# The experts' sums of the last chunk: from one VectorE instruction to ScalarE and GpSimd

## The chip, the cores and the metric

The kernel runs on one core of a Trainium2 chip. The metric is device time in microseconds (us) of one execution, smaller is better. Engines are named as the profile names them: PE (TensorE), DVE (VectorE), ACT (ScalarE), POOL (GpSimd), SP (SyncE, which here only issues DMAs). Each engine works through its own queue in order, and waits on semaphores for the others.

## The reference

Three stages. A top-32 attention (2 batches, 8 heads, 576 positions, head size 64) gives 1152 rows of 512. Then come four experts, all computed for every row and weighted by a normalised gate, and then a layer with three first matrices whose products are maximised:

```python
p = domain_probs / (domain_probs.sum(-1, keepdims=True) + 1e-09)
out = np.zeros((N, D))                      # N, D = 1152, 512; E = 4; F = 1024
for e in range(E):
    h = np.maximum(x @ w1[e], 0.0)
    out += p[:, e:e + 1] * (h @ w2[e])
...
h = np.maximum(np.maximum(x @ w1, x @ w2), x @ w3)     # d_ff = 768
return (h @ w_out).astype(np.float32)
```

The change is in the line `out += p * (h @ w2)`. The last stage's four matrices arrive as float64.

## The kernel before, in words

The 1152 rows are nine tiles of 128, in four chunks: `CHUNKS = [[0, 1], [2, 3], [4, 5], [6, 7, 8]]`. The work runs in eight phases, `PHASES`: the experts of chunks 0 to 3, then the last layer of chunks 0 to 3. The attention of later chunks goes on beside the first three expert phases. When the experts of chunk 3 (the last chunk, three tiles, N = 384 columns) run, it has ended.

**Experts.** An expert's 1024 hidden units are worked on in halves i = 0 to 7 (two halves to an expert). For each half PE makes two first products (`half1`, u = 0 and 1, 24 matmuls of 384 columns each into two PSUM banks); ACT takes them out with the ReLU into `hh`, DVE writes the remainder `hl` (L668, L670; every fourth goes over ACT and POOL, L661 to L663). Then `half2` multiplies with the second matrix: for each of the three tiles 12 matmuls of 512 columns into a PSUM tile `ps2` of the pool `po`, which has two buffers. So the third tile of a half (and the first tile of the next) can only begin when the buffer of two tiles earlier has been read out. The order on PE is first products of i+1, second products of i, and so on. Below, "step" is one such pair: 48 matmuls of 384 columns and 36 of 512.

What reads `ps2` out in the last chunk: for i = 0 ACT copies it with the gate's factor into `acc` (L692, three instructions). For i = 1 to 7 DVE does `acc = ps * gate + acc` in one instruction (L699), 3 x 7 = 21 of them. `ON_POOL_E = (0, 1)` keeps a third way (L693 to L696) switched off. In the chunks with two tiles both halves of an expert are added up in PSUM, and the same L699 runs once per expert and tile.

**Order of the instructions.** The read-outs are put on a list by `later()`; each later read-out first lets every waiting one issue its next stage (`tick`), so a read-out of two stages issues its second instruction when the next but one is put on the list. Nothing reorders afterwards: the order in which the program issues is the order on each engine.

**Weights.** Every 128x1024 block of weights is loaded by SP (L176), split by ACT into a high part `whi` (L225) and by POOL or DVE into the remainder `wlo` (L231). In the last chunk and the phases after it the blocks alternate: one on POOL (two instructions of 128x512), one on DVE (one of 128x1024). There are five buffers of each part; `weight()` splits up to four blocks ahead.

**Conversion.** Beside all this the four float64 matrices are turned into float32, in 48 pieces of 128x256 (`to_float32`). A piece takes two ACT instructions (L196, L197), three DVE instructions (L199, L202, L205), one POOL addition of int32 (L208), and an ACT-issued DMA that stores it (L213, `narrow`); five buffers circulate for the raw and five for the finished piece. The loads of the next phase's weights read what was stored.

**What sets how conversion and expert work interleave.** The program keeps two counters, `clock["dve"]` and `clock["pe"]`, of DVE and PE work issued so far. Per slot of the attention and conversion schedule, PE work is issued until it has caught up with the DVE work issued. Each L699 is counted there by `dve(DM)`, 0.07 + 512/960 = 0.60 us:

```python
                dve(DM)
                stages = [lambda: nc.vector.scalar_tensor_tensor(out=acc[ti], in0=ps, scalar=g, in1=acc[ti], op0=ALU.mult, op1=ALU.add)]
```

After the experts of chunk 3 comes the last layer of chunk 0 (phase 4), whose first products (216 matmuls of 256 columns) need the turned sums `x2h`, `x2l` of chunk 0 (L747 on PE, L752 on ACT, L753 on DVE) and the split weights.

Of the kernel before, what the change touches and what calls it, by code (L numbers as in the profile page):

```python
# [10 lines left out]
F32 = mybir.dt.float32  # L11
# [9 lines left out]
BEGIN, READY = 4, 4  # L21
SPLIT_K, SPLIT_Q = 8, 10
ON_POOL_H = 4
ON_POOL_E = (0, 1)
H_LAG, E_LAG = 0, 0
WAITING = 3
PAUSE = 0.8
# [23 lines left out]
def kernel(  # L51
# [15 lines left out]
    B, HP, D, _, S = k.shape  # L67
    NT, DM = out.shape
    E = gates.shape[2]
    P = 128  # L70
# [11 lines left out]
    MAXT = max(len(x) for x in CHUNKS)  # L82

    SLOTS = [[(t, b) for t in x for b in ((0, 1) if t == MIXED else (0 if t < MIXED else 1,))] for x in CHUNKS]
    MAXS = max(len(x) for x in SLOTS)
# [3 lines left out]
    kv = ctx.enter_context(tc.tile_pool(name="kv", bufs=2))  # L89
    qp = ctx.enter_context(tc.tile_pool(name="qp", bufs=2))  # L90
# [4 lines left out]
    ms = ctx.enter_context(tc.tile_pool(name="ms", bufs=2))  # L95
# [546 lines left out]
    def experts(n, c):  # L642
# [36 lines left out]
        def half2(i, ti, hs):  # L679
            begin, end = (not i % 2, i % 2 == 1) if whole else (True, True)  # L680
            if begin:
                outs[ti] = po.tile([P, DM], F32, tag="o", name="ps2")
            ps = outs[ti]
            assert {("h", n, i, 0), ("h", n, i, 1)} <= made
            yield from layer2(ps, [weight((c, "b", i, u), (c, "b", i, 0)) for u in range(2)], hs, N, ti, begin, end)
            if not end:
                return

            g = gate[:, tiles[ti], i // 2:i // 2 + 1]
            made_e[0] += 1  # L690
            if i < 1 + whole:
                stages = [lambda: nc.scalar.activation(out=acc[ti], in_=ps, func=AF.Copy, scale=g)]  # L692
            elif made_e[0] % ON_POOL_E[1] < ON_POOL_E[0]:  # L693
                tmp = ms.tile([P, 2 * MAXT * P], F32, tag="tm", bufs=2, name="tmp")[:, 0:DM]
                stages = [lambda: nc.scalar.activation(out=tmp, in_=ps, func=AF.Copy, scale=g),
                          lambda: nc.gpsimd.tensor_tensor(out=acc[ti], in0=acc[ti], in1=tmp, op=ALU.add)]  # L696
            else:
                dve(DM)
                stages = [lambda: nc.vector.scalar_tensor_tensor(out=acc[ti], in0=ps, scalar=g, in1=acc[ti], op0=ALU.mult, op1=ALU.add)]  # L699
            if i == 2 * E - 1:  # L700
                final = stages.pop()
                stages.append(lambda: [final(), made.add(("acc", c, ti))])
            later(*[lambda: None] * E_LAG, *stages)
# [213 lines left out]
```

## Time and profile before

| | us |
|---|---|
| median of the runs shown (3 runs, 794.56 to 802.54) | 795.2 |
| the profiled execution, own time | 795.39 |
| its span, first to last instruction | 793.6 |
| PE busy in the span | 737.1 (93%) |
| DVE busy | 666.1 (84%) |
| POOL busy | 557.5 (70%) |
| ACT busy | 492.8 (62%) |
| last chunk's experts, first to last matmul | 488.10 to 629.96 |

The own time is 1.8 us longer than the span. A PE that is busy need not be at its peak, since consecutive matmuls overlap in the records. The useful number is the distance between starts: about 0.17 us for 384 columns and 0.23 us for 512 in the last chunk.

### The profile page before, as it was taken

How to read it: one execution, taken by the hardware profiler on the slowest of the kernel's cores; microseconds unless marked ns; L12 is line 12 of the kernel's file. 1: busy time of each engine (PE TensorE's matmuls, PEld its weight loads, DVE VectorE, ACT ScalarE, POOL GpSimd, SP SyncE). 2: the span in 40 equal slices, each digit the busy share in tenths (PEclk: the TensorE clock that was granted, in tenths of full speed). 3: DMA queues.
4: the chain of work that ended last, by engine and by line, in shares of the span. 5: the costliest groups of instructions: out<-in, count | busy, mean ns of one | idle time of the engine just before them, and what ended most of it. 6: DMA issues, size and time to landing. Idle time of an engine off the chain costs nothing.

```text
span 793.6 us, 14150 instructions
## 1 busy us (share of the span) xinstructions
PE 737.1 (93%) x4942; PEld 656.4 (83%) x4942; DVE 666.1 (84%) x1242; ACT 492.8 (62%) x1027; POOL 557.5 (70%) x452
## 2 busy tenths in 40 slices
PE   3776799889999999999999999999999899999998
PEld 2554699788898988888888988889988797989996
DVE  6999999999999999999999996889999773434341
ACT  5666768577786776777777765755654444544541
POOL 2787988779888978778878785677465574655430
PEclk9976799999999999999999999999999999999999
DMA  3430155535555446354543465968877554656431
GB/s 99 119 108 4 52 166 153 173 112 165 161 178 154 141 146 176 99 162 132 158 133 130 136 196 169 282 220 269 248 248 243 167 171 174 213 186 208 166 104 41
DMA packets 50216, 126.26 MB, mean 159 GB/s; under 512 B 7904, under 2 KB 18144, under 8 KB 50144
## 3 DMA queue, kind: packets, MB, share of 16 engines
q1 hardware_dynamic: 41936, 116.69, 48.0%
q10 hardware_dynamic: 8208, 8.65, 3.1%
q8 instruction: 39, 0.64, 0.3%
q14 instruction: 33, 0.27, 0.1%
HBM read 116.67 MB, written 8.65 MB: 158 GB/s over the span
## 4 chain that ended last, share of the span: by engine, by line
DVE 44%; PE 33%; DMA 8%; issue 6%; POOL 4%; ACT 4%; SPq 1%; ACTq 0%; DVEq 0%; POOLq 0%
DVE m L372 16%; DVE work L374 14%; PE ps L590 8%; PE ps L592 8%; PE ps L591 8%; DVE p L392 6%; POOL wlo L231 3%; DMA raw<-in_w_dram 2%; ACT whi L225 2%; DMA raw<-narrow 2%; DVE h L670 2%; PE pso L592 1%; PE pso L590 1%; DMA raw<-in_m_dram 1%; PE pso L591 1%
## 5 line engine op out<-in xcount | busy, mean ns | idle before, releaser
L231 POOL TENSOR_TENSOR wlo<-raw,whi 128x512 fp32r<-128x512 f32 x272 | 374.9, 1406 | 140.2 <-ACT whi L225 129.0
L225 ACT ACTIVATE whi<-raw 128x1024 fp32r<-128x1024 f32 x176 | 182.8, 1057 | 76.2 <-PE ps L592 25.2
L590 PE MATMUL ps<-xl,whi 128*128 128x256 f32 (+1 forms) x512 | 154.2, 301 | 0.5 <-DVE h L670 0.5
L372 DVE MAX8 m<-work 128x8 f32<-128x576 f32 x216 | 154.4, 741 | 0.1
L592 PE MATMUL ps<-xh,wlo 128*128 128x256 f32 (+1 forms) x512 | 151.8, 296 | 0.0
L591 PE MATMUL ps<-xh,whi 128*128 128x256 f32 (+1 forms) x512 | 151.7, 296 | 0.0
L231 DVE TENSOR_TENSOR wlo<-raw,whi 128x1024 fp32r<-128x1024 f32 x40 | 57.4, 1435 | 76.5 <-ACT whi L225 71.9
L374 DVE MATCH_REPLACE8 work<-m,work 128x576 f32<-128x576 f32 x144 | 106.2, 738 | 0.0
L590 PEld LDWEIGHTS ps<-xl,whi 128*128 128x128 f32 x512 | 97.7, 191 | 1.6 <-DVE h L670 0.7
L591 PEld LDWEIGHTS ps<-xh,whi 128*128 128x128 f32 x512 | 97.8, 191 | 0.9
L592 PEld LDWEIGHTS ps<-xh,wlo 128*128 128x128 f32 x512 | 97.7, 191 | 0.0
L592 PE MATMUL ps<-x2h,wlo 128*128 128x256 f32 (+1 forms) x288 | 85.4, 297 | 0.8 <-DVE wlo L231 0.8
L590 PE MATMUL ps<-x2l,whi 128*128 128x256 f32 (+1 forms) x288 | 85.2, 296 | 0.0
L591 PE MATMUL ps<-x2h,whi 128*128 128x256 f32 (+1 forms) x288 | 85.2, 296 | 0.0
L590 PE MATMUL ps<-wlo,h 128*128 128x512 f32 x192 | 77.8, 405 | 0.0
L592 PE MATMUL ps<-whi,h 128*128 128x512 f32 x192 | 75.3, 392 | 0.0
L591 PE MATMUL ps<-whi,h 128*128 128x512 f32 x192 | 75.3, 392 | 0.0
L392 DVE SCALAR_TENSOR_TENSOR p<-s,m,p 128x576 f32<-128x576 f32 x57 | 73.4, 1288 | 0.0
L410 PE MATMUL psp<-ident,p 128*128 128x128 f32 x288 | 49.4, 299 | 24.1 <-POOL p L396 15.4
L351 PE MATMUL pss<-kT,ql 128*128 128x288 f32 x160 | 55.0, 358 | 13.5 <-DVE ql L295 7.5
L208 POOL TENSOR_TENSOR narrow<-narrow,raw 128x256 int32<-128x256 int32 x48 | 41.4, 863 | 33.7 <-DVE narrow L205 9.6
L410 PEld LDWEIGHTS psp<-ident,p 128*128 128x128 f32 x288 | 37.4, 153 | 30.3 <-POOL p L396 18.8
(104 smaller groups left out, 1682.1 us busy)
## 6 DMA issues: line engine op xcount, KB each, us to landing
raw<-in_w_dram SPq DMA_DIRECT2D x128, 512.0 KB, 3.8
raw<-narrow SPq DMA_DIRECT2D x48, 512.0 KB, 3.5
raw<-in_m_dram SPq DMA_DIRECT2D x36, 256.0 KB, 4.6
narrow<-narrow ACTq DMA_DIRECT2D x48, 128.0 KB, 3.9
kraw<-in_k_dram SPq DMA_DIRECT2D x14, 288.0 KB, 4.3
raw<-in_mo_dram SPq DMA_DIRECT2D x12, 256.0 KB, 4.0
vt<-in_v_dram SPq DMA_DIRECT2D x8, 288.0 KB, 4.3
out_dram<-ob ACTq DMA_DIRECT2D x9, 256.0 KB, 2.1
```

What stands on the lines that cost most here:

```text
L208: nc.gpsimd.tensor_tensor(out=out.bitcast(I32), in0=out.bitcast(I32), in1=last, op=ALU.add)
L225: nc.scalar.activation(out=hi, in_=raw, func=AF.Copy)
L231: on.tensor_tensor(out=lo[:, x], in0=raw[:, x], in1=hi[:, x].bitcast(F32), op=ALU.subtract)
L351: nc.tensor.matmul(ps[:, 0:SH], lhsT=l, rhs=r, start=i == 0, stop=i == len(mm) - 1)
L372: nc.vector.max(m[:, 8 * r:8 * r + 8], src)
L374: nc.vector.match_replace(out=self.w[j], in_to_replace=m[:, 8 * r:8 * r + 8], in_values=src, imm_value=NEG)
L392: nc.vector.scalar_tensor_tensor(out=p, in0=s, scalar=kth, in1=p, op0=ALU.is_ge, op1=ALU.mult, accum_out=total)
L410: nc.tensor.transpose(ps[:, r * P:(r + 1) * P], self.p[:, part, part * TAIL + r * P:part * TAIL + (r + 1) * P], ident)
L590: nc.tensor.matmul(ps, lhsT=lh, rhs=rl, start=first, stop=False)
L591: nc.tensor.matmul(ps, lhsT=lh, rhs=rh, start=False, stop=False)
L592: nc.tensor.matmul(ps, lhsT=ll, rhs=rh, start=False, stop=last)
L670: lambda: [nc.vector.scalar_tensor_tensor(out=hl[:, g], in0=ps, scalar=0.0, in1=hh[:, g].bitcast(F32), op0=ALU.max, op1=ALU.subtract) for ...
```

## The change

For the last chunk (`not whole`), i = 1 to 7, the one DVE instruction is replaced by two. ACT takes the product out of PSUM with the gate's factor into `tmp`, and POOL adds `tmp` to `acc`. `tmp` alternates between two tiles, those in which the attention loaded its raw q and raw k (one buffer each). `dve(DM)` is not called on this path.

```diff
@@ -21,7 +21,6 @@
 BEGIN, READY = 4, 4
 SPLIT_K, SPLIT_Q = 8, 10
 ON_POOL_H = 4
-ON_POOL_E = (0, 1)
 H_LAG, E_LAG = 0, 0
@@ -690,8 +689,10 @@
             made_e[0] += 1
             if i < 1 + whole:
                 stages = [lambda: nc.scalar.activation(out=acc[ti], in_=ps, func=AF.Copy, scale=g)]
-            elif made_e[0] % ON_POOL_E[1] < ON_POOL_E[0]:
-                tmp = ms.tile([P, 2 * MAXT * P], F32, tag="tm", bufs=2, name="tmp")[:, 0:DM]
+            elif not whole:
+
+                tmp = (qp.tile([P, 2, MAXS * P], F32, tag="qraw", bufs=1, name="tmp") if made_e[0] % 2 else
+                       kv.tile([P, 2, S], F32, tag="kraw", bufs=1, name="tmp")).rearrange("p a n -> p (a n)")[:, 0:DM]
                 stages = [lambda: nc.scalar.activation(out=tmp, in_=ps, func=AF.Copy, scale=g),
                           lambda: nc.gpsimd.tensor_tensor(out=acc[ti], in0=acc[ti], in1=tmp, op=ALU.add)]
             else:
```

PE's order stays as it was, row for row. On the others, two kinds of thing move: the read-out itself, and, because the counter of DVE work now grows more slowly, the conversion's pieces relative to the expert work. Line numbers of the changed kernel are one lower than before up to the change, and one higher behind it.

The queue of ACT at the read-outs of i = 1. `whi` is a weight's high part, `narrow` and `raw64` a piece of the conversion, `hh` a hidden block, `ps2` the product. Before:

```order
L668 ACTIVATE hh_6730<-ps1_6717 128x384
L213 DMA narrow3_101<-narrow_6664 128x256
L196 ACTIVATE narrow_6802<-raw64_6734 128x256
L197 ACTIVATE raw64_6734<-raw64_6734 128x256
L213 DMA narrow3_101<-narrow_6689 128x256
L225 ACTIVATE whi_6815<-raw_6697 128x1024
L225 ACTIVATE whi_6822<-raw_6746 128x1024
```

And now:

```order
L667 ACTIVATE hh_6730<-ps1_6717 128x384
L212 DMA narrow3_101<-narrow_6664 128x256
L195 ACTIVATE narrow_6793<-raw64_6734 128x256
L196 ACTIVATE raw64_6734<-raw64_6734 128x256
L696 ACTIVATE tmp_6770<-ps2_6741,gate_95 128x512
L212 DMA narrow3_101<-narrow_6689 128x256
L195 ACTIVATE narrow_6820<-raw64_6763 128x256
L196 ACTIVATE raw64_6763<-raw64_6763 128x256
L696 ACTIVATE tmp_6796<-ps2_6773,gate_95 128x512
L224 ACTIVATE whi_6826<-raw_6697 128x1024
L224 ACTIVATE whi_6833<-raw_6746 128x1024
L696 ACTIVATE tmp_6823<-ps2_6800,gate_95 128x512
```

The three read-outs now stand in ACT's queue, the first behind a store of the conversion and a piece's two instructions, and the two `whi` stand behind the second.

POOL's queue in the same step, from the remainder of the weight that is loaded as `raw_6697` on. Before:

```order
L231 TENSOR_TENSOR wlo_6816<-raw_6697,whi_6815 128x512 x2
L208 TENSOR_TENSOR narrow_6767<-narrow_6767,raw64_6685 128x256
L231 TENSOR_TENSOR wlo_6868<-raw_6820,whi_6867 128x512 x2
L208 TENSOR_TENSOR narrow_6802<-narrow_6802,raw64_6734 128x256
L208 TENSOR_TENSOR narrow_6846<-narrow_6846,raw64_6763 128x256
L208 TENSOR_TENSOR narrow_6893<-narrow_6893,raw64_6798 128x256
L208 TENSOR_TENSOR narrow_6921<-narrow_6921,raw64_6842 128x256
L663 TENSOR_TENSOR hl_6913<-raw_6914,hh_6912 128x768
```

And now:

```order
L697 TENSOR_TENSOR acc_6341<-acc_6341,tmp_6770 128x512
L230 TENSOR_TENSOR wlo_6827<-raw_6697,whi_6826 128x512 x2
L697 TENSOR_TENSOR acc_6342<-acc_6342,tmp_6796 128x512
L207 TENSOR_TENSOR narrow_6793<-narrow_6793,raw64_6734 128x256
L697 TENSOR_TENSOR acc_6343<-acc_6343,tmp_6823 128x512
L230 TENSOR_TENSOR wlo_6884<-raw_6831,whi_6883 128x512 x2
L207 TENSOR_TENSOR narrow_6820<-narrow_6820,raw64_6763 128x256
L207 TENSOR_TENSOR narrow_6861<-narrow_6861,raw64_6789 128x256
L207 TENSOR_TENSOR narrow_6909<-narrow_6909,raw64_6816 128x256
L207 TENSOR_TENSOR narrow_6950<-narrow_6950,raw64_6857 128x256
L662 TENSOR_TENSOR hl_6926<-raw_6927,hh_6925 128x768
L207 TENSOR_TENSOR narrow_6966<-narrow_6966,raw64_6905 128x256
```

Three additions are new in the step, between the remainders and the pieces of the conversion.

The end of POOL's conversion, from the remainder of phase 4's first weight on. Before:

```order
L231 TENSOR_TENSOR wlo_7744<-raw_7602,whi_7743 128x512 x2
L208 TENSOR_TENSOR narrow_7680<-narrow_7680,raw64_7619 128x256
L208 TENSOR_TENSOR narrow_7715<-narrow_7715,raw64_7647 128x256
L231 TENSOR_TENSOR wlo_7823<-raw_7748,whi_7822 128x512 x2
L208 TENSOR_TENSOR narrow_7766<-narrow_7766,raw64_7676 128x256
L231 TENSOR_TENSOR wlo_7871<-raw_7827,whi_7870 128x512 x2
L208 TENSOR_TENSOR narrow_7797<-narrow_7797,raw64_7711 128x256
L208 TENSOR_TENSOR narrow_7852<-narrow_7852,raw64_7762 128x256
L231 TENSOR_TENSOR wlo_7956<-raw_7875,whi_7955 128x512 x2
L208 TENSOR_TENSOR narrow_7895<-narrow_7895,raw64_7793 128x256
L797 TENSOR_TENSOR h_7820<-tm_7821,h_7820 128x512
L208 TENSOR_TENSOR narrow_7935<-narrow_7935,raw64_7848 128x256
```

(one more piece follows). And now:

```order
L230 TENSOR_TENSOR wlo_7825<-raw_7669,whi_7824 128x512 x2
L207 TENSOR_TENSOR narrow_7787<-narrow_7787,raw64_7730 128x256
L207 TENSOR_TENSOR narrow_7820<-narrow_7820,raw64_7756 128x256
L697 TENSOR_TENSOR acc_6341<-acc_6341,tmp_7852 128x512
L697 TENSOR_TENSOR acc_6342<-acc_6342,tmp_7876 128x512
L697 TENSOR_TENSOR acc_6343<-acc_6343,tmp_7896 128x512
L230 TENSOR_TENSOR wlo_7905<-raw_7829,whi_7904 128x512 x2
L207 TENSOR_TENSOR narrow_7864<-narrow_7864,raw64_7783 128x256
L230 TENSOR_TENSOR wlo_7945<-raw_7909,whi_7944 128x512 x2
```

Of the 48 pieces, eight stood behind that weight before and three do now: five have moved ahead of phase 4.

## Rows read from the trace of the kernel before

**Rows 1.** Busy time of each engine in stretches of the span, granted clock, DMA share.

```profile
core 0: us, PE busy (x) PEld busy (x) DVE busy (x) ACT busy (x) POOL busy (x), PEclk, DMA share, GB/s
522.41:541.16 18.75, 17.00 (x85) 15.01 (x85) 16.80 (x29) 11.14 (x22) 11.73 (x11) 1.00 0.84 277
...
557.90:574.64 16.74, 16.74 (x85) 15.09 (x85) 15.59 (x25) 9.12 (x18) 9.05 (x9) 1.00 0.80 248
608.12:629.96 21.84, 19.19 (x81) 15.23 (x81) 16.00 (x23) 8.53 (x15) 12.08 (x10) 0.92 0.57 180
629.96:655.88 25.92, 25.92 (x218) 25.91 (x216) 19.04 (x23) 12.07 (x20) 18.41 (x15) 1.00 0.58 194
```

**Rows 2.** Timeline of PE: the matmuls after its two long waits, and the transposes.

```profile
529.92 0.50 PE L590 MATMUL ps<-wlo,hh 128*128 128x512 f32 x1 [1.75 <-DVE acc L699]
...
616.52 1.03 PE L747 MATMUL pst<-ident,acc 128*128 128x128 f32 x8
...
625.80 0.80 PE L590 MATMUL ps<-wlo,hh 128*128 128x512 f32 x1 [2.65 <-DVE acc L699]
```

**Rows 3.** Groups by line, 541.16 to 608.12: count | busy, mean ns | idle before, releaser.

```profile
L231 POOL TENSOR_TENSOR wlo<-raw,whi 128x512 fp32r<-128x512 f32 x16 | 21.6, 1372 | 6.8 <-ACT whi L225 6.8
L208 POOL TENSOR_TENSOR narrow<-narrow,raw 128x256 int32<-128x256 int32 x20 | 17.0, 848 | 18.3 <-DMA narrow<-narrow 4.4 <-DVE narrow L205 3.8 <-DMA raw<-in_m_dram 2.6
L225 ACT ACTIVATE whi<-raw 128x1024 fp32r<-128x1024 f32 x16 | 16.8, 1053 | 15.1 <-PE ps L592 15.0
L231 DVE TENSOR_TENSOR wlo<-raw,whi 128x1024 fp32r<-128x1024 f32 x9 | 11.0, 1222 | 2.6 <-ACT whi L225 2.6
L699 DVE SCALAR_TENSOR_TENSOR acc<-ps,gate,acc 128x512 f32<-128x512 f32 x12 | 8.9, 740 | 0.0
L663 POOL TENSOR_TENSOR hl<-raw,hh 128x768 fp32r<-128x768 f32 x2 | 3.8, 1914 | 0.0
```

**Rows 4.** Timeline of DVE and POOL, 549 to 555: start, duration.

```profile
549.46 1.27 DVE L231 TENSOR_TENSOR wlo<-raw,whi 128x1024 fp32r<-128x1024 f32 x1 [0.31 <-ACT whi L225]
...
551.63 1.40 DVE L205 SCALAR_TENSOR_TENSOR narrow<-raw,narrow 128x256 uint32<-128x256 uint32 x1
552.95 1.50 DVE L199 SCALAR_TENSOR_TENSOR raw<-narrow,raw 128x256 f32<-128x256 f32 x1
...
549.61 1.73 POOL L208 TENSOR_TENSOR narrow<-narrow,raw 128x256 int32<-128x256 int32 x1
551.30 2.88 POOL L231 TENSOR_TENSOR wlo<-raw,whi 128x512 fp32r<-128x512 f32 x2
```

**Rows 5.** Single lines: duration in ns min/median/max, first and last start.

```profile
L231 POOL TENSOR_TENSOR wlo<-raw,whi x38: 1269/1345/2289, 502.9 to 654.2; 128x512 fp32r<-128x512 f32 x38
L208 POOL TENSOR_TENSOR narrow<-narrow,raw x48: 731/810/1757, 487.0 to 649.2; 128x256 int32<-128x256 int32 x48
L231 DVE TENSOR_TENSOR wlo<-raw,whi x40: 1208/1226/2311, 484.1 to 770.5; 128x1024 fp32r<-128x1024 f32 x40
L199 DVE SCALAR_TENSOR_TENSOR raw<-narrow,raw x48: 412/419/1523, 480.1 to 645.4; 128x256 f32<-128x256 f32 x48
L202 DVE TENSOR_SCALAR narrow<-raw x48: 275/726/1390, 480.6 to 645.9; 128x256 uint32<-128x256 uint32 x48
L205 DVE SCALAR_TENSOR_TENSOR narrow<-raw,narrow x48: 408/426/2031, 480.9 to 647.1; 128x256 uint32<-128x256 uint32 x48
L699 DVE SCALAR_TENSOR_TENSOR acc<-ps,gate,acc x39: 732/739/751, 169.2 to 630.2; 128x512 f32<-128x512 f32 x39
L692 ACT ACTIVATE acc<-ps,gate x9: 677/691/707, 131.7 to 515.4; 128x512 f32<-128x512 f32 x9
```

**Rows 6.** Timeline of ACT before the read-outs of i = 1.

```profile
529.03 0.43 ACT L196 ACTIVATE narrow<-raw 128x256 f32<-128x256 f32 x1 [2.06 <-DMA narrow<-narrow]
529.36 0.42 ACT L197 ACTIVATE raw<-raw 128x256 int32<-128x256 uint32 x1
```

**Rows 7.** Timeline of POOL: the remainder of phase 4's first weight.

```profile
618.78 3.54 POOL L231 TENSOR_TENSOR wlo<-raw,whi 128x512 fp32r<-128x512 f32 x2 [5.55 <-ACT whi L225]
```

## The prediction, made before the changed kernel ran

> **What bounds the kernel now.** I read the stretches of the last chunk first [rows 1]. A step without a wait takes 16.74 us on PE (557.90 to 574.64), at full granted clock. The steps from 541.16 to 608.12, four of them, 66.96 us, run at that pace, so PE sets the time there. PE loses time at two places of the stretch that the change touches, and both times it waits for L699, DVE's read-out: 1.75 us before 529.92 and 2.65 us before 625.80 [rows 2]. The second costs more than the wait. Its stretch took 21.84 us at a clock of 0.92 [rows 1], against 16.74 for a step plus at most 1.03 for the eight transposes in it [rows 2]: 4.1 us lost. The first step took 18.75: 2.0 lost. So the most that an ideal read-out can win here is 6.1 us, 0.8% of 795.
>
> Next, what DVE and POOL do to each other, since the change takes work from one and gives it to the other. DVE's L205 and L199 take 0.41 us at their shortest [rows 5], but 1.40 and 1.50 where POOL's pair of subtractions runs (551.30 to 554.18) [rows 4]. That pair took 2.88 instead of 2 x 1.27 = 2.54, 0.34 more, about one DVE instruction that slipped between its halves. POOL's L208 took 1.73 instead of 0.73 while DVE's L231 ran until 550.73, and ended 0.61 after it [rows 4, 5]. So these instructions exclude each other, nearly for their whole length. L699 does not take part: 39 times between 732 and 751 ns [rows 5], whatever POOL did. It reads one operand from PSUM. That is the point of this case: the instruction removed is one that got along with POOL, and the one added on POOL (two fp32 operands in SBUF, 128x512, the form of L231) is one that shuts DVE's conversion and subtractions out.
>
> How full is this shared time already? Prices of what each holds: POOL's minima [rows 5]; DVE's minima less 0.07, since 0.34 of L205's 0.41 showed up in POOL's pair. Four steps from 541.16 [rows 3]: POOL 16 x 1.27 + 20 x 0.73 + 2 x 1.91 = 38.7. DVE 20 pieces x (0.34 + 0.34 + 0.21) + 8 subtractions x 1.14 = 26.9 (the ninth in the row lies almost wholly before the stretch). Together 65.6 of 66.96 us: 98%. PE just keeps its pace there, with nothing to spare next to it.
>
> The page "SBUF — State Buffer" of the Trainium skill, section "SBUF: two separate sides", calls the port pair of DVE and GpSimd an exclusive lock, held for the whole instruction. By that rule, with whole durations, the four steps would need 38.7 + 31.7 = 70.4 us, more than they took; so the overlap of about 0.07 that the row shows is kept, and the end worked out below would lie some 7 us later by the rule.
>
> **The change part by part.** *Removed:* 21 x 0.74 = 15.5 us of DVE [rows 5]. It frees DVE's queue, but none of the shared time, as shown.
>
> *Added on ACT:* 21 x 0.69 = 14.5 us, at the price of L692, the same operation [rows 5], 2.1 us a step. ACT is busy 9.1 of 16.74 us in a step [rows 1] and in four steps waited 15.0 us for PE before splitting a weight [rows 3]; 3.8 a step, more than a read-out holds up the splits behind it. I cost it at nothing; without that cover it would be up to 14.5. The first read-out of a step is no earlier than before, though: at i = 1 it stands behind the piece whose L197 ends at 529.78 [rows 6], so it begins where DVE's began, and the first wait of PE stays.
>
> *Added on POOL:* 21 additions. No add of this form is in the trace; L231's 1.27 to 1.35 [rows 5] has the same operands and shape with another output type. Ends: 0, if additions fit into POOL's idle time beside DVE, and 21 x 1.35 = 28; I take 1.27 each, 26.7, all of it shared time. Nobody waits for the sums themselves before chunk 3's turn two phases later. But behind each addition stand remainders and pieces, and behind those PE.
>
> *Moved:* without `dve(DM)` the counter of DVE work grows by 0.60 x 21 = 12.7 us less, so pieces come earlier relative to PE: 11 in two steps instead of 10, and five of the eight that stood behind phase 4's first weight now stand ahead of it. Each holds 0.73 + 0.89 = 1.62 of shared time: 8.1 us more before phase 4. Their DMAs move with them (SP's raw loads, ACT's stores). I cost these moves at nothing, because the splits wait for PE and almost never for a load (15.0 of 15.1 us) [rows 3].
>
> *The new wait:* `tmp` has two tiles, so the third read-out of a step waits for the first addition. Behind it in ACT's queue stand a store, a piece, the next weight's split and the next hidden block. And ACT's stores wait for POOL's L208, with the first read-out behind one. A late POOL holds ACT, and ACT holds PSUM; PE has one tile's time, 2.7 us, before it feels that.
>
> *Sum.* In a step the shared demand goes from 16.4 to (65.6 + 12 x 1.27 + 2 x 1.62) / 4 = 21.0 us, against 16.74 of PE. The lag adds up until phase 4, whose first product needs its first weight's remainder. From about 529, where the first addition comes due (behind L197 and one read-out, with one piece still ahead of it on POOL), to that remainder the new order holds on POOL 18 additions, 22 halves of remainders, 30 pieces and 3 hidden remainders: 40 x 1.27 + 30 x 0.73 + 3 x 1.91 = 78.4. Beside it DVE holds 30 pieces x 0.89 + 10 x 1.14 = 38.1. Together 116.5 us; at a filling of 98%, 118.9: the remainder is ready at 647.9. Before, phase 4's first products began at 629.96 [rows 1], the remainder done at 622.3 [rows 7]. That is 17.9 us later. Behind it, up to phase 4's third weight, the queue holds 10.7 us more (three additions, two pieces, two subtractions) against 5.8 of PE for two weights, which could add 5; against that, phase 4 is rid of five pieces and ran 25.92 us anyway, so I leave both out. The profiled execution took 795.39, 0.2 above the median: 795.4 + 17.9 = **813 us**.
>
> Bounds: before, the same stretch (529 to 622.3) held, by the same count without additions and with 25 pieces, 85.6 us in 93.3, a filling of 92%, waits included. At 92% the remainder comes at 655.6: +26. If the prices are 7% too high, at 98%, it is +9. So +9 to +26: 804 to 821.
>
> **Rivals.** *Relief.* DVE was late at both waits, and POOL is idle for 67.0 - 42.4 = 24.6 us in four steps [rows 3], 6.1 a step, while the additions want 3.8. If they ran in that idle time without holding DVE up, the loss at 625.80 would go (4.1) and the first stay: 791; with both gone 789. It decides where an addition meets DVE: L699's 732 to 751 ns say that DVE's PSUM work goes on beside POOL, and that fraction speaks for it; the 98% speaks against. The skill's page "Perfetto Trace Analysis", section "Optimizing Scalar/DVE Operations", has both halves: move work from a saturated DVE to Scalar or even GPSIMD, but expect that between those two it might not help. By its first half it is this 791; the rows of the stretched L205 bear out the second. Chance 0.14, a fifth of it beyond 1%.
>
> *Absorbed.* The first remainder was ready 7.6 us before its use [rows 7], there are five buffers of each weight part, and the hidden blocks have a whole step. If the lag stays below that, or more overlaps than I price, PE waits little: 4 less to 8 more, 796. That the new order isn't carried out is no case: 21 rows leave DVE, 21 come on ACT and on POOL. Chance 0.18.
>
> *Chained queues.* ACT stands behind POOL's pieces in every step, PE waits at every third tile, and its granted clock falls to the lower of its two levels, 1.2 GHz, as it did for part of the stretch with 0.92 [rows 1], where the first matmul after the wait took 0.80 us against 0.50 after the other wait [rows 2]. Then the filling drops under 92%: 821 to 835, say 827. Chance 0.11.
>
> **How the numbers follow.** Forecast 0.57 (804 to 821), chained 0.11, absorbed 0.18, relief 0.14. A range from 793 to 828 leaves out most of relief, half of the chained case and a little of the absorbed one, some 0.2. A measurement of this kernel tells about 1% (8 us) from no change: slower by more 0.57 + 0.11 - 0.01 = 0.67, within 0.18 + 0.11 + 0.01 = 0.30, faster 0.03.
>
> **What would show it.** In the changed profile: L697's additions near 1.3 us each and L205, L199 more often at 1.4 than 0.42 (shared time). DVE's busy share not falling by 15 us, because waiting counts as busy. Steps of 19 to 22 us between 541 and phase 4; phase 4's first product near 648; PE waiting for remainders, or for ACT's read-outs behind POOL. Wrong, if steps stay at 16.7 although POOL is busy over 13 us in each, or if an addition leaves L205 at 0.41 beside it.

## The result, and the profile after

The changed kernel took 805.97 us (median of 4 runs, 803.51 to 807.46) and the kernel before, in runs beside them, 797.14 (4 runs, 794.56 to 802.54): a ratio of 1.0102, with a 95% interval of 1.0064 to 1.014. It is slower by 1.0%. The forecast was 813, with a range of 793 to 828, which also holds the time before. The profiled execution took 805.2 us, its span 803.4.

Busy time of the engines, from the first part of the page of the changed kernel:

```profile
PE 742.8 (92%) x4942; PEld 659.8 (82%) x4942; DVE 673.8 (84%) x1221; ACT 505.1 (63%) x1048; POOL 587.5 (73%) x473
```

POOL grew by 30.0 us, of which the 21 additions are 29.1. DVE, which lost 15.5 us of work, grew by 7.7: its instructions that wait for POOL count as busy (L204 takes 1.39 to 1.41 us beside an addition, 0.41 at its shortest).

The new instructions, by the view of the tile `tmp` (duration in ns min/median/max, first and last start):

```profile
L696 ACT ACTIVATE tmp<-ps,gate x21: 660/683/700, 528.2 to 642.4; 128x512 f32<-128x512 f32 x21
L697 POOL TENSOR_TENSOR acc<-acc,tmp x21: 1293/1348/1486, 531.9 to 643.8; 128x512 f32<-128x512 f32 x21
```

The steps from 523 on, by the view of stretches, and three pieces of PE's long stops; they answer to [rows 1]:

```profile
core 0: us, PE busy (x) PEld busy (x) DVE busy (x) ACT busy (x) POOL busy (x), PEclk, DMA share, GB/s
523.46:540.20 16.74, 16.74 (x86) 15.01 (x85) 14.83 (x21) 10.58 (x21) 12.15 (x11) 1.00 0.73 237
540.20:554.93 14.73, 10.21 (x37) 7.82 (x37) 13.70 (x19) 8.64 (x16) 10.69 (x11) 0.88 0.75 241
554.93:571.68 16.75, 16.75 (x86) 15.10 (x84) 16.54 (x21) 9.55 (x20) 13.95 (x12) 1.00 0.70 210
571.68:595.09 23.41, 19.39 (x86) 16.83 (x85) 20.94 (x26) 13.86 (x26) 19.05 (x17) 0.87 0.66 221
595.09:612.07 16.98, 16.98 (x85) 15.33 (x84) 15.88 (x21) 11.09 (x21) 13.29 (x12) 0.98 0.74 238
612.07:629.02 16.95, 16.95 (x86) 14.96 (x85) 16.64 (x19) 10.51 (x23) 14.15 (x13) 1.00 0.72 222
629.02:641.12 12.10, 9.68 (x45) 7.36 (x43) 11.21 (x14) 6.12 (x12) 10.90 (x10) 1.00 0.38 124
...
550.48:554.93 4.45, 4.45 (x12) 3.50 (x13) 3.63 (x4) 3.19 (x5) 4.04 (x4) 0.62 0.70 220
589.80:595.09 5.29, 5.29 (x13) 4.18 (x14) 3.67 (x3) 3.34 (x5) 5.29 (x5) 0.50 0.52 181
```

Only some steps are longer, and there only the second products are. The stretch 540.20 to 554.93 holds second products alone, 36 of them, and took 14.73 us where 8.40 is the pace without a wait. The next such block, the last part of the row from 571.68, took 15.07 (580.02 to 595.09), and the one behind the transposes 11.31 (629.81 to 641.12). The stretches between them ran at a step's 16.74 to 16.98, with POOL busy for 12.2 to 14.2 us in each. PE's waits there, from its timeline (in brackets the idle time before, and who ended it); they answer to [rows 2]:

```profile
550.48 0.50 PE L589 MATMUL ps<-wlo,hh 128*128 128x512 f32 x1 [4.52 <-ACT tmp L696]
...
589.80 0.80 PE L589 MATMUL ps<-wlo,hh 128*128 128x512 f32 x1 [4.02 <-ACT tmp L696]
...
636.63 0.50 PE L589 MATMUL ps<-wlo,hh 128*128 128x512 f32 x1 [0.99 <-ACT tmp L696]
641.12 0.39 PE L589 MATMUL ps<-x2l,whi 128*128 128x256 f32 x1 [1.43 <-DVE x2l L754]
```

PE waits for ACT's read-out now, not for DVE's. A long wait costs more than itself: the third tile's products behind it, a third of a block, took 4.45 and 5.29 us at a granted clock of 0.62 and 0.50, against 8.40 / 3 = 2.80 at full clock. So the first long block's loss, 14.73 - 8.40 = 6.33, is 4.52 of waiting, 1.65 of slow products, and 0.16 of the ordinary kind.

Where the time went, by PE's first matmul of each phase. Section A runs from the start of the last chunk's products to that of phase 4's, section B from there to that of phase 5's:

| | A | B | sum |
|---|---|---|---|
| before | 488.10 to 629.96: 141.9 | to 666.95: 37.0 | 178.9 |
| after | 489.49 to 641.12: 151.6 | to 677.59: 36.5 | 188.1 |

The sum grew by 9.2 us, as the median by 8.8. All of it lies in A: the three long blocks lose 6.3 + 6.7 + 2.9 = 15.9 us, where before two places lost 6.1 [rows 1, 2].

What held ACT before the first long wait, from the timelines of ACT (ACTq is its issuing of DMAs) and POOL; the rows answer to [rows 4, 6]:

```profile
540.40 1.06 ACT L224 ACTIVATE whi<-raw 128x1024 fp32r<-128x1024 f32 x1 [2.31 <-POOL acc L697]
...
544.05 0.36 ACTq L212 DMA_DIRECT2D narrow<-narrow  x1
544.52 0.44 ACT L195 ACTIVATE narrow<-raw 128x256 f32<-128x256 f32 x1 [2.29 <-POOL narrow L207]
...
545.66 0.36 ACTq L212 DMA_DIRECT2D narrow<-narrow  x1
548.37 0.43 ACT L195 ACTIVATE narrow<-raw 128x256 f32<-128x256 f32 x1 [2.33 <-DMA narrow<-narrow]
...
549.75 0.67 ACT L696 ACTIVATE tmp<-ps,gate 128x512 f32<-128x512 f32 x1
```

```profile
536.74 1.48 POOL L697 TENSOR_TENSOR acc<-acc,tmp 128x512 f32<-128x512 f32 x1
...
539.06 1.33 POOL L697 TENSOR_TENSOR acc<-acc,tmp 128x512 f32<-128x512 f32 x1
540.36 2.92 POOL L230 TENSOR_TENSOR wlo<-raw,whi 128x512 fp32r<-128x512 f32 x2
543.23 0.79 POOL L207 TENSOR_TENSOR narrow<-narrow,raw 128x256 int32<-128x256 int32 x1
544.82 0.82 POOL L207 TENSOR_TENSOR narrow<-narrow,raw 128x256 int32<-128x256 int32 x1 [0.79 <-DVE narrow L204]
```

Read backwards: the read-out that PE waits for begins at 549.75. Ahead of it in ACT's queue stands a piece of the conversion whose L195 waits until 548.37 for the store of the piece five earlier, which holds its buffer. Counted by the pieces, that is the store issued at 544.05, directly behind the L207 that POOL ended at 544.02 (the median from issue to landing of these stores is 4.4 us); ACT had stood 2.29 us for that L207 already. On POOL it stands behind two additions (536.74 and 539.06) and a weight's remainder. So ACT's read-out is late because the conversion is, and a part of that is POOL's additions. How large a part the rows alone don't tell.

### The profile page after: what moved, and what is told of

It is laid out like the page before. It is cut to its first block, busy times and chain, and to the rows that moved or that the text cites. A ratio compares the mean times of both kernels' runs of the same rounds, so it can differ in the third digit from the quotient of the medians.

```text
span 803.4 us, 14168 instructions
## 1 busy us (share of the span) xinstructions
PE 742.8 (92%) x4942; PEld 659.8 (82%) x4942; DVE 673.8 (84%) x1221; ACT 505.1 (63%) x1048; POOL 587.5 (73%) x473
## 4 chain that ended last, share of the span: by engine, by line
DVE 41%; PE 30%; DMA 11%; issue 6%; ACT 6%; POOL 5%; SPq 2%; ACTq 0%; DVEq 0%; POOLq 0%
DVE m L371 14%; DVE work L373 13%; PE ps L589 7%; PE ps L591 7%; PE ps L590 7%; DVE p L391 6%; DMA narrow<-narrow 4%; POOL wlo L230 3%; ACT whi L224 3%; DMA raw<-in_w_dram 2%; DVE h L669 2%; SPq L247 2%; PE pso L591 2%; PE pso L589 1%; PE pso L590 1%
## 5 line engine op out<-in xcount | busy, mean ns | idle before, releaser
L230 DVE TENSOR_TENSOR wlo<-raw,whi 128x1024 fp32r<-128x1024 f32 x40 | 62.8, 1571 | 81.1 <-ACT whi L224 67.3
L409 PE MATMUL psp<-ident,p 128*128 128x128 f32 x288 | 49.3, 299 | 23.5 <-POOL p L395 15.3
L207 POOL TENSOR_TENSOR narrow<-narrow,raw 128x256 int32<-128x256 int32 x48 | 40.2, 842 | 26.4 <-DVE narrow L204 10.7
```

Of the source, the lines that this page charges most:

```text
L207: nc.gpsimd.tensor_tensor(out=out.bitcast(I32), in0=out.bitcast(I32), in1=last, op=ALU.add)
L230: on.tensor_tensor(out=lo[:, x], in0=raw[:, x], in1=hi[:, x].bitcast(F32), op=ALU.subtract)
L409: nc.tensor.transpose(ps[:, r * P:(r + 1) * P], self.p[:, part, part * TAIL + r * P:part * TAIL + (r + 1) * P], ident)
```

## The experiments

Each kernel was timed against runs of the kernel before beside it, whose medians were 795.89 to 797.67; ratios carry 95% intervals. A ratio is taken over all the runs and can differ from that of the medians by 0.2%. A and B are the sections above, from one profiled execution each, which can lie off its kernel's median: 2.3 us above it with memsets, 3.4 above in last_half_only, 4.3 below in store_on_sp.

| run | median, us (runs) | ratio to before | A | B |
|---|---|---|---|---|
| the change | 805.97 (4) | 1.0102 (1.0064 to 1.014) | 151.6 | 36.5 |
| noadd_uncounted | 797.55 (12) | 1.0009 (0.9986 to 1.0033) | 144.9 | 35.1 |
| half_add | 799.15 (12) | 1.0016 (0.999 to 1.0042) | 145.0 | 35.1 |
| memset_uncounted | 803.45 (6) | 1.0094 (1.0067 to 1.0121) | 150.6 | 36.8 |
| dveadd_uncounted | 801.71 (10) | 1.0061 (1.0039 to 1.0083) | 148.5 | 36.1 |
| dve_uncounted | 801.06 (12) | 1.0069 (1.0044 to 1.0093) | 149.3 | 35.0 |
| add_counted | 807.76 (6) | 1.0125 (1.0089 to 1.0161) | 143.6 | 44.1 |
| noadd_counted | 802.29 (12) | 1.0056 (1.0027 to 1.0085) | 140.9 | 43.1 |
| last_half_only | 799.93 (12) | 1.0046 (1.0025 to 1.0067) | 141.6 | 43.5 |
| ring6_change | 807.3 (6) | 1.0111 (1.0073 to 1.0149) | 152.1 | 37.0 |
| ring6_before | 797.57 (12) | 1.0003 (0.9976 to 1.0031) | 142.3 | 36.9 |
| store_on_sp | 810.93 (6) | 1.018 (1.0138 to 1.0221) | 156.1 | 37.0 |
| hidden_on_dve | 804.8 (6) | 1.0097 (1.0067 to 1.0127) | 148.4 | 39.6 |

### Is it the additions? (noadd_uncounted)

The change without its second stage. The last chunk's products are taken out but not added, so seven eighths of its sums are left out.

```diff
-                stages = [lambda: nc.scalar.activation(out=tmp, in_=ps, func=AF.Copy, scale=g),
-                          lambda: nc.gpsimd.tensor_tensor(out=acc[ti], in0=acc[ti], in1=tmp, op=ALU.add)]
+                stages = [lambda: nc.scalar.activation(out=tmp, in_=ps, func=AF.Copy, scale=g), lambda: None]
```

> The changed kernel without POOL's 21 additions: the sums of chunk 3 keep only the first half's product, and the others are read out into tmp and dropped. Order of the pieces as in the changed kernel. Shared time: the loss is gone, 0 to 4 us below before, no wait of PE over 1 us for a read-out. Order of the pieces: 6 to 8 us above before. ACT's place: 8 above before.

797.55 us, 1.0009: the kernel before again. The additions are the loss, and 21 read-outs on ACT together with the pieces moved ahead cost nothing that this measurement tells. PE still waited four times for `tmp`, 8.3 us in all against 9.5 in the changed kernel, but no wait was longer than 2.92. The products behind the two longest ran at a clock of 1.00, by the view of stretches:

```profile
532.02:534.93 2.91, 2.91 (x12) 2.36 (x13) 1.82 (x4) 2.91 (x5) 1.46 (x2) 1.00 0.78 239
586.87:589.75 2.88, 2.88 (x12) 2.35 (x13) 1.24 (x1) 2.88 (x5) 2.88 (x3) 1.00 0.83 298
```

So PE's waiting alone does not make up the difference. Section A as one stretch, of the kernel before, the changed kernel and the one without additions:

```profile
488.10:629.96 141.86, 136.82 (x681) 122.25 (x680) 127.85 (x188) 81.13 (x156) 90.65 (x80) 0.99 0.76 242
...
489.49:641.12 151.63, 140.38 (x681) 124.09 (x679) 143.20 (x181) 93.57 (x181) 119.16 (x101) 0.97 0.72 228
...
489.76:634.61 144.85, 136.27 (x682) 120.97 (x680) 125.02 (x182) 92.58 (x181) 94.19 (x82) 1.00 0.73 239
```

PE was idle (length less busy time) for 5.0, 11.3 and 8.6 us. Of the 6.8 us between the last two rows 2.7 are idle time and 4.1 are busy time, at a granted clock of 0.97 against 1.00. This split holds for one execution each: the mean granted clock over all runs, 0.958 with the change and 0.962 without additions, does not tell the two apart, so how the loss divides between waiting and slow products in a typical run stays open.

### Is it POOL's time, or what POOL does to DVE? (memset_uncounted, half_add)

POOL's addition becomes two memsets of `tmp`, of 768 and 640 columns, together about as long (21 pairs took 29.2 us in all, the 21 additions 29.3; the sums are left out as above):

```diff
+                both, tmp = tmp[:, 0:768], tmp[:, 0:DM]
...
-                          lambda: nc.gpsimd.tensor_tensor(out=acc[ti], in0=acc[ti], in1=tmp, op=ALU.add)]
+                          lambda: [nc.gpsimd.memset(both, 0.0), nc.gpsimd.memset(both[:, 0:640], 0.0)]]
```

> The changed kernel with each of POOL's 21 additions replaced by two memsets of tmp (768 and 640 columns; the sums of chunk 3 keep only the first half's product). The page of before has a memset of 128x1 at 0.10 and of 128x128 at 0.21 us, so an estimate of about 0.74 + 0.63 = 1.37 us for the two, as long as an addition, in the same place of POOL's queue, waiting for the same read-out, but reading nothing from SBUF. Shared time (additions shut DVE out): as without additions, 0 to 2 us above before, and DVE's pieces not stretched beside the memsets. POOL's queue alone (an addition is 1.3 us in front of remainders and pieces, whatever DVE does): as the changed kernel, 7 to 9 above before.

803.45 us, 1.0094: the loss is there in full. The memset pair held POOL as long as an addition, and DVE's two-operand instructions went on beside it. A pair from POOL's timeline and the DVE instruction beside it, in the kernel with memsets:

```profile
539.92 1.46 POOL L698 MEMSET tmp<- 128x768 f32 x2
...
540.84 0.43 DVE L204 SCALAR_TENSOR_TENSOR narrow<-raw,narrow 128x256 uint32<-128x256 uint32 x1
```

And an addition in the changed kernel, with what DVE began beside it:

```profile
539.28 1.39 DVE L204 SCALAR_TENSOR_TENSOR narrow<-raw,narrow 128x256 uint32<-128x256 uint32 x1
```

L204 took 0.41 to 0.43 in the 13 cases in which it began beside a memset, and 1.39 to 1.41 in the 7 in which it began beside an addition (539.06 to 540.39 in POOL's timeline above is one). The sum over a piece, by the groups of lines from 523 to 640 (count | busy, mean ns), first of the changed kernel and then of the one with memsets:

```profile
L204 DVE SCALAR_TENSOR_TENSOR narrow<-raw,narrow 128x256 uint32<-128x256 uint32 x35 | 32.4, 926 | 0.9
L201 DVE TENSOR_SCALAR narrow<-raw 128x256 uint32<-128x256 uint32 x34 | 28.4, 834 | 0.7
L198 DVE SCALAR_TENSOR_TENSOR raw<-narrow,raw 128x256 f32<-128x256 f32 x34 | 26.3, 773 | 0.0
```

```profile
L201 DVE TENSOR_SCALAR narrow<-raw 128x256 uint32<-128x256 uint32 x34 | 29.8, 877 | 0.7
L204 DVE SCALAR_TENSOR_TENSOR narrow<-raw,narrow 128x256 uint32<-128x256 uint32 x35 | 22.5, 642 | 0.9
L198 DVE SCALAR_TENSOR_TENSOR raw<-narrow,raw 128x256 f32<-128x256 f32 x35 | 19.6, 559 | 1.0 <-ACT narrow L195 1.0
```

A piece's three DVE instructions took 2.53 us in the changed kernel and 2.08 with memsets. The same groups of the kernel before, 522 to 630, give 0.63 + 0.66 + 0.82 = 2.10. So with memsets DVE was rid of what the additions do to it, and nothing that can be told of the loss was won back. What costs is the time that POOL's queue gives to the additions. PE's waits had the same form: 2.49 us before 532.78 and 4.01 before 590.33, each ended by ACT's read-out and followed by 12 products at a granted clock of 0.62.

Then half of that time: the addition on 256 of the 512 columns (the other half of the sums is left out).

```diff
-                          lambda: nc.gpsimd.tensor_tensor(out=acc[ti], in0=acc[ti], in1=tmp, op=ALU.add)]
+                          lambda: nc.gpsimd.tensor_tensor(out=acc[ti][:, 0:256], in0=acc[ti][:, 0:256], in1=tmp[:, 0:256], op=ALU.add)]
```

> The changed kernel with each of POOL's additions on 256 of the 512 columns only (the other half of chunk 3's sums keeps the first half's product). An addition should take about 0.73 us, as L208 of that shape, instead of 1.35: 13 us of POOL's queue less. POOL's time in its queue is the cost (what the memsets pointed to): between the run without additions and the change, 2 to 5 us above before. That an addition must wait for its read-out at all, whatever its length: as the changed kernel, 8 above before.

799.15 us, 1.0016: no loss that can be told, though the wait for `tmp` and all 21 additions are there, each of 0.82 us at the median, by the view of the tile:

```profile
L697 POOL TENSOR_TENSOR acc<-acc,tmp x21: 735/820/927, 533.2 to 637.1; 128x256 f32<-128x256 f32 x21
```

Half-way between no addition and the whole would be 1.0056, above the interval. So the price doesn't look proportional: POOL has room for about half of what the change gives it, and the second half costs 0.8 to 0.9% (1.0102 or 1.0094 against 1.0016).

### The addition on DVE (dveadd_uncounted)

```diff
-                          lambda: nc.gpsimd.tensor_tensor(out=acc[ti], in0=acc[ti], in1=tmp, op=ALU.add)]
+                          lambda: nc.vector.tensor_tensor(out=acc[ti], in0=acc[ti], in1=tmp, op=ALU.add)]
```

> The changed kernel with the 21 additions on DVE instead of POOL: ACT reads out, DVE adds tmp to acc from SBUF (about 0.6 us as an estimate from L797's 0.69 of the same shape). Shared time: half the port time of an addition on POOL, so between the run without additions and the change: 2 to 5 us above before. POOL's queue: as without additions, 0 to 2 above before.

801.71 us, 1.0061. The addition takes 0.69 us there at the median, less than the 0.74 of the instruction that the change removed [rows 5], and POOL is free of it. It still costs: ACT's read-outs waited 13.1 us in all for DVE's additions (5 waits, up to 3.5 us, by the view of waits), since those stand in DVE's order behind the conversion. An addition in either queue puts ACT behind it.

### What the moved pieces do (dve_uncounted, add_counted, noadd_counted)

The kernel before with L699 as it is, but not counted in the last chunk, so that the pieces come early as in the change:

```diff
-                dve(DM)
+                if whole:
+                    dve(DM)
```

> The kernel before, with the last chunk's read-outs not counted as DVE work: DVE reads out in one instruction as before, but the pieces stand as early as in the changed kernel. Shared time: five pieces more (7 us) ahead of phase 4, no additions: 0 to 3 us above before. Order of the pieces: the whole loss, 8 us above before. ACT's place: before.

801.06 us, 1.0069: A is 7.4 us longer than before, B 2.0 shorter. With DVE's own read-out behind more pieces, PE's waits for it are there again (the longest 2.95 us before 532.72 and 3.44 before 635.14).

The change with the count put back, with and without additions (the second leaves out the sums as above):

```diff
             elif not whole:
-
+                dve(DM)
                 tmp = (qp.tile([P, 2, MAXS * P], F32, tag="qraw", bufs=1, name="tmp") if made_e[0] % 2 else
```

> The change, with the counter of DVE work raised for each read-out as before, so that the conversion's 48 pieces stand where they stood (eight behind phase 4's first weight, not three); ACT's read-outs and POOL's 21 additions stay. Shared time of POOL and DVE (my theory): the additions' 27 us of port time stay and only five pieces (7 us) leave the stretch, so most of the loss stays: 3 to 6 us above before, PE still waits for ACT's read-outs. Order of the pieces (first rival: the pieces that came earlier hold up ACT's queue): back to before, within 2 us. ACT's place (second rival: a read-out in ACT's queue is late whatever POOL adds): as the changed kernel, 8 above before.

> As the run without additions (the same part of the sums left out), but with the pieces where they stood before. Shared time: 2 to 5 us below before, since DVE's late read-outs are gone too. Order of the pieces: 0 to 4 below before. ACT's place: 8 us above before.

807.76 and 802.29 us. With eight pieces left behind phase 4's first weight the last chunk is as fast as before or nearly so (A 143.6 and 140.9), and B is longer, 44.1 and 43.1 against 37.0. The eight pieces alone don't explain that, since the kernel before leaves the same eight there. Against it noadd_counted has another read-out (and sums left out) and the same order of instructions otherwise, and it is 0.56% slower: with the pieces in their old places ACT's read-outs are not free. The moved pieces with DVE's read-outs aren't either (0.69%, dve_uncounted). Only the two together cost nothing that can be told (noadd_uncounted). Between the two kernels of this pair the additions cost 0.7%. With ACT's read-outs the moved pieces are no loss: they cost 4.0 us in A and give back 8.0 in B without additions, 8.0 and 7.6 with them.

### Only where DVE was late (last_half_only)

The places where PE waited for DVE before were i = 1 and i = 7 [rows 2]. This kernel takes the new way for i = 7 alone, counted; the rest is as before.

```diff
-            elif not whole:
-
+            elif not whole and i == 2 * E - 1:
+                dve(DM)
                 tmp = (qp.tile([P, 2, MAXS * P], F32, tag="qraw", bufs=1, name="tmp") if made_e[0] % 2 else
```

> Only the read-outs of the last half (i = 7, three of 21) go over ACT and POOL, counted as DVE work; the other 18 stay on DVE. That is where PE lost 4.1 us before. Shared time: three additions where the conversion thins out cost nothing, PE's wait of 2.65 us and the slow clock behind it go: 2 to 4 us below before. ACT's place in the queue is what counts: the wait stays, before within 2 us.

799.93 us, 1.0046: not faster. The wait at i = 7 is gone, and its block took 8.48 us (623.37 to 631.85) instead of the 12.65 that it took before. The longest stop now comes in phase 4's second products, 36 us after that block. PE's timeline in this kernel, and the stretch of those products:

```profile
663.30 0.50 PE L591 MATMUL pso<-whi,h 128*128 128x512 f32 x1 [1.72 <-POOL h L798]
...
667.70 0.79 PE L589 MATMUL pso<-wlo,h 128*128 128x512 f32 x1 [3.20 <-ACT h L797]
```

```profile
657.83:675.32 17.49, 11.99 (x46) 8.84 (x45) 4.50 (x6) 6.27 (x9) 6.24 (x5) 0.80 0.49 173
```

And what ACT and then DVE wait for there, from their timelines:

```profile
663.21 1.06 ACT L224 ACTIVATE whi<-raw 128x1024 fp32r<-128x1024 f32 x1 [3.29 <-DMA raw<-narrow]
...
667.01 0.63 ACT L797 ACTIVATE h<-tm 128x512 fp32r<-128x512 f32 x1 [2.75 <-DVE tm L794]
```

```profile
664.36 1.23 DVE L230 TENSOR_TENSOR wlo<-raw,whi 128x1024 fp32r<-128x1024 f32 x1 [6.90 <-ACT whi L224]
665.50 1.48 DVE L794 TENSOR_TENSOR tm<-ps,tm 128x512 f32<-128x512 f32 x2
```

Read backwards again: PE at 667.70 waits for `h`, L797 for DVE's L794, which began at 665.50 because in DVE's queue it stands behind a weight's remainder; that waited 6.90 us for the weight's split on ACT, and that for the load of what the conversion had stored. POOL's part of the last pieces had ended at 657.46. The second products took 16.70 us (658.62 to 675.32), where 8.3 is the pace without a wait. So the time won at i = 7, 4.2 us, is more than given back: B is 6.5 us longer. In the kernel before PE waits for the same `h` for only 1.42 us (before 661.10).

The additions aren't the reason: noadd_counted has none, and PE stops there as long (1.71 us before 663.06, 3.29 before 667.54; B 43.1). What both have in common against the kernel before are the last half's read-outs in ACT's queue, ahead of a weight's split. Here, from ACT's timeline:

```profile
632.11 0.69 ACT L696 ACTIVATE tmp<-ps,gate 128x512 f32<-128x512 f32 x1 [1.89 <-PE ps L591]
632.70 1.05 ACT L224 ACTIVATE whi<-raw 128x1024 fp32r<-128x1024 f32 x1
...
641.60 1.06 ACT L224 ACTIVATE whi<-raw 128x1024 fp32r<-128x1024 f32 x1 [3.95 <-DMA raw<-narrow]
```

The split at 632.70 stands behind a read-out that waits for PE's tile. It begins 9.5 us after the first `x2h` (623.22); in the kernel before the same split began 6.3 us after it (623.48, 617.16). Two weights later ACT waits 3.95 us for a load of what the conversion stored. That these 3 us grow into the 6.5 of B fits the order of the queues, but was not tried apart.

This kernel also had a longer wait at i = 1 than before (3.53 us before 533.51); that one differs from run to run, so A isn't the sum of the two.

### Three ways to loosen the chain (ring6_change, ring6_before, store_on_sp, hidden_on_dve)

In the changed kernel ACT's L195 waited 15.8 us in all for earlier stores, by the view of waits, 520 to 680 (us in total, times, longest):

```profile
ACT narrow L195 <- DMA narrow<-narrow: 15.8, 12, 2.3
POOL narrow L207 <- DVE narrow L204: 10.3, 8, 2.1
PE ps L589 <- ACT tmp L696: 9.5, 3, 4.5
```

First six buffers for the finished piece instead of five, in the change and in the kernel before:

```diff
-        out = at.tile([P, 1024 // WIDE], F32, tag="s1", bufs=AHEAD_S, name="narrow")
+        out = at.tile([P, 1024 // WIDE], F32, tag="nw", bufs=6, name="narrow")
...
-            s = at.tile([P, 2, SH], F32, tag="s%d" % j, bufs=AHEAD_S, name="s")
+            s = at.tile([P, 2, SH], F32, tag="s%d" % j, bufs=(AHEAD_S, 3)[j], name="s")
```

> The changed kernel with six buffers for the finished pieces of the conversion instead of five (in a place of their own; the attention's second score buffer goes from five to three to make room). Same order on every engine. Loop of buffers (ACT's L195 waits for the store of the piece five earlier, 15.8 us in twelve waits, and the read-out stands behind it): PE's waits for read-outs shrink by half or more, 4 to 8 us below the changed kernel. POOL's queue without that loop: within 2 us of the changed kernel, 8 above before.

> The same buffers in the kernel before. Loop of buffers: DVE's late read-outs come with pieces that wait in that loop, so PE's first wait goes or shrinks: 1 to 4 us below before. POOL's queue: before within 2 us. If three score buffers hold up the attention, both runs with six buffers are slower by the same amount, and the start of the last chunk's products shows it.

1.0111 and 1.0003: no difference. The waits for stores went, and others of the same size took their place, on the loads of the raw piece:

```profile
ACT narrow L195 <- DMA raw<-in_m_dram: 14.5, 10, 2.8
```

Five buffers aren't the cause; the wait named in the trace is only the last link of a chain that is late.

Then the finished piece's store issued by SP instead of ACT:

```diff
-        nc.scalar.dma_start(out=narrow[wide[n // WIDE][0]][:, n % WIDE * 1024 // WIDE:(n % WIDE + 1) * 1024 // WIDE], in_=out)
+        nc.sync.dma_start(out=narrow[wide[n // WIDE][0]][:, n % WIDE * 1024 // WIDE:(n % WIDE + 1) * 1024 // WIDE], in_=out)
```

> The changed kernel with the conversion's stores issued by SP instead of ACT, so that ACT's queue no longer stops at a store until POOL has finished the piece. Chained queues (a late POOL holds ACT at the stores, and ACT holds PSUM): PE's waits for ACT's read-outs shrink, 3 to 6 us less than the changed kernel, if SP's weight loads don't come late instead. Shared time without that chain: as the changed kernel, 8 above before.

810.93 us, 1.018: worse. PE's longest wait is 6.24 us (before 588.79), and L195 waited 38.5 us in all for stores. So ACT was not freed: it now stood at L195, and this run doesn't tell what its stop at the store costs. That SP's loads now stand behind stores that wait for POOL fits this, but was not tried apart.

Last, POOL freed of every fourth hidden block in the last chunk (L662), since the long waits lie in the steps that have one:

```diff
-            if ON_POOL_H and not count % ON_POOL_H:
+            if ON_POOL_H and whole and not count % ON_POOL_H:
```

> The changed kernel, but in the last chunk every hidden block's remainder stays on DVE (no fourth block over ACT and POOL). That takes 1.85 us of POOL's queue and about 1.3 of ACT's out of every second step, the very steps in which PE waited for a read-out, and gives DVE two instructions of 0.55 us there. POOL's time in its queue is the cost: the waits in those steps shrink, 4 to 8 us below the changed kernel, level with before or better. A step on DVE's side (its pieces come late, since it gets more work): as the changed kernel or slower, 8 to 10 above before.

804.8 us, 1.0097: no better. The waits moved to other steps (2.81 us before 563.44, 2.05 before 600.90, 1.65 before 630.92), and phase 4's first block waited for a remainder:

```profile
643.02 0.39 PE L591 MATMUL ps<-x2h,wlo 128*128 128x256 f32 x1 [2.16 <-POOL wlo L230]
```

So POOL's 1.85 us for a hidden block have a part in where the stops fall, but taking them away won nothing. No kernel here beat the kernel before.

## Why the prediction was right, and where its size was off

*Direction and range: right.* 806 lies in 793 to 828, and the loss is caused by the additions, as the forecast has it (noadd_uncounted). The 8.8 us are just over the 8 that the prediction wanted for telling a loss, and the range is wide enough to hold the time before too.

*What bounds before: right.* PE waited for DVE's read-out at two places.

*Two terms put at nothing: right together, by luck.* The forecast costed the 14.5 us on ACT at nothing, and the moved pieces at nothing too. Together they are (noadd_uncounted, 1.0009), but each by itself is not: ACT's read-outs with the pieces in their old places cost 0.56% (noadd_counted), the moved pieces with DVE's read-outs 0.69% (dve_uncounted). The prediction gave no reason why one should make up for the other.

*The first wait: open.* It was expected to stay. In the changed kernel's profile it did not show (523.46 to 540.20 took 16.74), with memsets it was 2.49, without additions 2.59, so one profile says little of that place.

*The additions' duration: right.* 1.27 forecast, 1.29 to 1.49 measured, and L204 at 1.39 to 1.41 beside them. DVE's busy time did not fall, as forecast.

*The mechanism, "all of it shared time": this step failed.* The instructions do exclude each other, but that isn't what the time is lost to. Memsets of the same length took that exclusion off L204 and L198 and left the loss at 1.0094. The forecast added DVE's and POOL's prices into one demand. The runs show a queue of POOL's own, with room for additions of half the length (1.0016) and not of the whole.

On this the Trainium skill says, in "SBUF — State Buffer", section "SBUF: two separate sides", that a DVE instruction with two SBUF inputs is shut out only by a GpSimd instruction that reads SBUF; the trace agrees (0.41 to 0.43 beside a memset, 1.39 to 1.41 beside an addition). "Perfetto Trace Analysis", section "Optimizing Scalar/DVE Operations", warns that moving work between those two might not help because of the port; the outcome agrees, and the memsets speak against the port as the reason here.

*The sum: +17.9 us forecast at phase 4's first product, +9.7 measured* (A 151.6 against 141.9). This is the term that was mis-sized. The prediction has a bound of +9 for prices 7% too high (its own working gives +9.6), and that the result lies there is luck: what A grew by is PE idle for 6.2 us more and, for the rest, mostly products at the lower clock, and the sum has no term for the clock. The sum gave 116.5 us of demand from 529 to the end of the first remainder of phase 4; POOL's timeline in the changed kernel shows that remainder from 634.74 on, 3.52 us long, so done at 638.26. That answers to [rows 7] and is 9.6 us before the forecast 647.9:

```profile
634.74 3.52 POOL L230 TENSOR_TENSOR wlo<-raw,whi 128x512 fp32r<-128x512 f32 x2
```

It was also not what released phase 4. PE's first product there waited for DVE's `x2l`, at 641.12.

*The steps of 19 to 22 us: wrong in shape.* The forecast spread the lag over all steps. The two steps from 540.20 to 580.02 took 39.8 us together and the two from there to 620.41 took 40.4, against 33.5 without a wait and 42.0 forecast, but all of it fell on one step of each pair. The text named steps that stay at 16.7 with POOL busy over 13 us as what would make it wrong; three of the stretches above are that (16.75, 16.98 and 16.95, with POOL busy for 13.95, 13.29 and 14.15).

*The rivals.* The chained queues describe the place better than the forecast does: PE stops for ACT's read-out, ACT for the conversion behind POOL, the granted clock falls to 0.62 and 0.50 of full. Only the size was about a third or less of what that rival gave it (+9 instead of +26 to +40). Relief fell twice. The whole change brings the additions' loss. At i = 7 alone it does take the wait away, and phase 4's second products then wait (B 43.5 instead of 37.0).

*What stays open.* Why the stops fall in some steps and not in others, and which link between ACT, DVE, POOL and the store is the tight one: four tries at single links (six buffers, SP's stores, hidden blocks, the addition on DVE) moved the stops or made them longer, and none came back to the time before. Also open is why ACT's read-outs and the moved pieces each cost something and together nothing. Effects under some 0.3% are below what these runs tell: the cost of those two together may be anything between -0.1% and +0.3%.

## What to carry to other kernels

In a chain of small steps that crosses three in-order queues, the idle time of a queue over a stretch overstates the room in it: here POOL was idle for 23.5 of 117.7 us (523.46 to 641.12) while the additions cost 1%. To tell a shared port from a queue's own time, put an instruction of equal length in place that leaves the other engine's instructions alone, and one of half the length; two runs spoke against what a careful sum of the port's time had made likely. Before removing a wait, look for what is next late in the same queues: at i = 7 the wait went, and phase 4 lost more than it had cost. And two terms put at nothing should be tried apart as well as together: here each alone cost over half a percent.

## What the runs showed of the hardware that was not expected

A GpSimd memset leaves DVE's two-operand instructions alone, a GpSimd addition does not: 0.41 to 0.43 us against 1.39 to 1.41 for the same L204. It does not leave L201 alone, DVE's instruction with one operand: five times it began inside a memset and took 0.51 to 0.59 instead of 0.28 at its shortest; the seven that began inside an addition took 1.19 to 1.28.

A memset of 128x768 and one of 128x640 take 1.43 to 1.46 us together, an addition of 128x512 from 1.29.

A wait of PE of 4 us was followed by 12 products at 0.62 or 0.50 of the full clock, the lower level being half. That added 1.6 to 2.5 us to each such wait, while waits of 2.59 and 2.92 in the kernel without additions added nothing (granted clock 1.00). The length of the wait alone doesn't decide it: with memsets a wait of 2.49 was followed by 4.40 us of such products at 0.62, and in the kernel before the wait of 2.65 [rows 2] by 4.16 us, at 0.66.
